# A fused attention, Fourier mix and MLP kernel: the place and time of the mix sums, and the weight steps of one attention turn

## The chip, the cores and the metric

One Trainium2 chip, one core. The metric is device time in microseconds of one launch, lower is better. Of several runs the median is given; one execution is profiled.

## What is computed

Attention with a bias that a small network makes of the distance between positions, then a two-dimensional Fourier transform whose real part is added, a normalisation and an MLP. Batch 4, 8 heads, 576 positions, head size 64, so 512 features; 2048 hidden units.

```
scores = q @ k.T / 8 + bias                     # bias = relu(x @ w1 + b1) @ w2, x from |i - j| and i
x  = softmax(scores) @ v                        # heads side by side: 4 x 576 x 512
u  = x + real(fft(fft(x, axis=1), axis=2))
un = (u - mean(u)) / sqrt(var(u) + 1e-6)        # over the 512 features
out = u + relu(un @ w_ch1) @ w_ch2
```

## The kernel before, in words

Everything is float32; products are made of high and low parts of about 12 bits each (`h` and `l` in tile names), three matmuls for one exact product: hi·hi, hi·lo, lo·hi (`PROD`).

**Attention** (to about 339 us) runs in 16 turns, one for a pair of heads and a batch. Within a turn the order of PE, DVE and ACT is written out by hand in a list of steps, `ORDER`, for all turns but the second (n = 1), which has a list of its own, `SECOND`, and the end, which has `TAIL`. POOL and the DMA queue of SP are ordered by the scheduler that builds the program; a queue runs strictly in order. A step's letter names its work, its digit a block, and a prime each turn that it lags: S scores on PE (`s`), D largest score on DVE (line 290), X exponential on ACT (`p`), T and R transposes on PE into a bank of PSUM (`t`, two banks), VT and VR their evacuation to `pt` (on ACT, or DVE for VR1'), A the products with v on PE (`o`).

W0 to W3 and U0 to U3 turn one 512 KB block of each of the two MLP weight matrices, which arrive as 64-bit floats in `raw`, into float32, one block of each in a turn: W0/U0 on ACT (line 164, `wf`/`uf`), 1 to 3 on DVE (lines 165 to 167), and behind step 3 a store to DRAM (`w_d`, lines 552 and 553). The next turn's `raw` loads are issued on SP when the buffers are free. `load(n)` loads `kT` and `qT` (line 189) when POOL has read the old ones into `kh`, `kl` and `qs` (lines 209, 213).

`keep_bias` (line 326) stores finished bias rows to DRAM (`bias_d`, line 330), six DMAs a call. The last calls, of blocks held back in `later`, stand behind turn n = 0.

**Fourier mix** of a batch b (class `Mix`): sums and differences of rows, `pq` (line 654), and of columns, `ge` (lines 656 and 658), c = 0 for sums and c = 1 for differences; `ge` is split into `gh` and `gl`; PE transforms along the positions (`zp`, line 674, ten matmuls of 320 columns for c and d each, of which part is interleaved) and along the features (`abp`); the result is added to x. For b = 0 all this stands in `TAIL`. For b = 1 to 3 it is part of the stream `pieces`, which is mixed with the dense matmuls of batch b − 1. For b = 1 the sums are made on POOL, otherwise on DVE.

**Dense** (349 to 783 us): `norm` makes the scaled tiles `un`, four of 128x512 (line 773); `flip` transposes them on PE (`ut`, line 787) and splits them into `uh` on ACT (line 789) and `ul` on DVE (line 790). Then for each of 16 blocks f, `up(f)`: splits w1 and w2 into `w1h`, `w1l`, `w2h`, `w2l` (h on ACT, l on POOL), 12 matmuls of 512 columns into `hp` (line 898) and a relu that is split into `hh` and `hl`; `down(f)`: 12 matmuls into the four `acc` (line 912). `end` adds `acc` to x (line 918) and stores. Batch b + 1 is normalised inside batch b; its four transposes stand between the last `down` matmuls of batch b. In the profile batch 0 begins at 349 us, batches 1, 2 and 3 take over near 450, 547 and 645 us, and the matmuls of the two remaining tiles come last, after 722 us. What the scheduler can make early it may put far ahead: before the change the sums of batch 2 were made at 359 to 372 us, inside batch 0.

`un`, `uh` and `ul` live in the pool `unp`, one buffer for each name; `pq` and `ge` of batches 1 to 3 have the pool `fgp`. A tile of the same name waits until the old one is read.

Of the kernel before, what the change touches and what calls it, by code (L numbers as in the profile page):

```python
# [9 lines left out]
F32 = mybir.dt.float32  # L10
# [9 lines left out]
DM, FF, HID = 512, 2048, 32  # L20
P = 128
# [33 lines left out]


SECOND = """
S1 D1 S2 T10' D2 S4 T00' VT10' T01' D4 VT00' VT01' S8' S3 T11' VT11' D8' X8' T02' D3 S6 Q0' VT02' D6 S0 R1'
R0' VR1' X3 VR0' D0 S7 S8 U0 T13' T12' W0 A0' D7 X6 W1 VT13' W2 W3 S5 T04' VT12' T03' D8 U1 Q1' A1' X7 X0
VT03' VT04' X1 D5 U2 U3 X5 A2'  # L60
""".split()


# [69 lines left out]
def body(ctx, tc, a, out):  # L133
    nc = tc.nc
# [270 lines left out]
    with ExitStack() as st:  # L405
# [212 lines left out]
        class Mix:  # L618
# [5 lines left out]
            def buffers(self, c):  # L624
                b = self.b
                if b:
                    pq = fgp.tile([P, 2, DM], F32, tag="pq", name="pq")
                    ge = fgp.tile([P, 3, 256], F32, tag="ge", name="ge")
                    gh = fgp.tile([P, 3, 256], F32R, tag=f"gh{c}", name="gh")
                    gl = fgp.tile([P, 2, 256], F32R, tag=f"gl{c}", name="gl")  # L630
                    self.pq, self.ge[c], self.g[c] = pq, (ge[:, 0:2], ge[:, 2]), (gh, gl)
                    return
# [245 lines left out]
            eng.tensor_tensor(l, src, h.bitcast(F32), ALU.subtract)  # L878
            return h, l

        def dense(ut, tiles, store):
            n = len(tiles)
            N = P * n
            acc = [tps.tile([P, 512], F32, tag="t", name="acc") for t in range(2)]
# [3 lines left out]
            hs, w2s = {}, {}  # L888

            def up(f):  # L890
                wh, wl = split(w1[f // 4][:, f % 4], "w1", nc.gpsimd)
                wf = w2p.tile([P, DM], F32, tag="w2f", name="w2f")
                nc.sync.dma_start(wf, w2_d[f])
                w2s[f] = split(wf, "w2", nc.gpsimd if n == 4 else nc.vector)
                ps = hps.tile([P, 512], F32, tag="h", name="hp")
                mm = [(kb, i, j) for kb in range(4) for i, j in PROD]
                for i, (kb, wi, ui) in enumerate(mm):
                    nc.tensor.matmul(  # L898
                        ps[:, :N], (wh, wl)[wi][:, P * kb:P * kb + P], ut[ui][:, kb, :N],
                        start=i == 0, stop=i == len(mm) - 1)  # L900
# [120 lines left out]
```

## Time and profile before

| | |
|---|---|
| runs | 788.43, 788.58, 784.47 us; median 788.43 |
| profiled execution | 784.86 us, span 783.0 us |
| PE busy | 758.1 us, 97% of the span |
| DVE, ACT, POOL busy | 433.7 (55%), 435.1 (56%), 354.1 us (45%) |
| chain that ended last | PE 88% |
| granted TensorE clock, mean | 0.99 |

The span runs from the first to the last instruction; the execution's time is 1.9 us longer. The chain is followed back from the last instruction to whatever released it, so PE's share of it is the share of time in which nothing but PE set the pace.

### The profile page before, as it was taken

The page shows a single profiled execution, that of the slowest core. Times are in us where ns is not written, and L with a number is a line of the kernel's source. Part 1 is how long each engine was busy: PE and PEld are TensorE (multiplying, and loading weights), DVE is VectorE, ACT ScalarE, POOL GpSimd, SP SyncE. Part 2 cuts the span into 40 slices and gives each one's busy share as a digit, 9 for nine tenths or more (in the row PEclk, how much of TensorE's full clock was granted, in tenths as well). Part 3 has the DMA queues.
Part 4 walks back from the last instruction along what each step waited for, and adds up shares of the span by engine and source line. Part 5 has one row for each costly group of instructions (what it writes and reads, how often), then busy time and mean ns, then how long its engine had stood idle before and what let it go on. Part 6 is the DMA issues. An engine that isn't in the chain of part 4 may idle for free.

```text
span 783.0 us, 13209 instructions
## 1 busy us (share of the span) xinstructions
PE 758.1 (97%) x4786; PEld 617.4 (79%) x4786; DVE 433.7 (55%) x958; ACT 435.1 (56%) x898; POOL 354.1 (45%) x299
## 2 busy tenths in 40 slices
PE   6999899999999999979999999999999999999997
PEld 3567678887788877848888888888888888888896
DVE  7996787987877877587471232713237132111433
ACT  7995888788987888434333333334333342333453
POOL 0003556554663644256554434644355444445442
PEclk9999999999999999979999999999999999999999
DMA  8988989989879743631211121112211112111321
GB/s 220 238 222 228 254 235 297 298 227 283 243 204 284 204 135 92 208 110 28 66 32 50 43 94 54 40 41 64 72 54 41 41 54 95 43 53 54 119 90 61
DMA packets 59488, 103.16 MB, mean 132 GB/s; under 512 B 8768, under 2 KB 28864, under 8 KB 58304
## 3 DMA queue, kind: packets, MB, share of 16 engines
q1 hardware_dynamic: 58672, 98.99, 44.1%
q0 software_dynamic: 288, 3.02, 1.2%
q8 instruction: 37, 0.61, 0.3%
q10 hardware_dynamic: 464, 0.33, 0.1%
q14 instruction: 27, 0.22, 0.1%
HBM read 78.58 MB, written 21.07 MB: 127 GB/s over the span
## 4 chain that ended last, share of the span: by engine, by line
PE 88%; DVE 3%; ACT 3%; DMA 3%; SPq 2%; issue 1%; ACTq 0%; DVEq 0%
PE hp L898 25%; PE acc L912 25%; PE s L272 10%; PE o L462 10%; PE t L441 7%; PE bps L391 4%; PE zp L674 2%; PE abp L693 2%; DMA raw<-m 2%; SPq L330 1%; ACT p L298 1%; PE t L493 1%; DVE un L773 1%; PE ut L787 1%; PE t L431 1%
## 5 line engine op out<-in xcount | busy, mean ns | idle before, releaser
L904 DVE SCALAR_TENSOR_TENSOR hl<-hp,hh 128x512 fp32r<-128x512 f32 (+1 forms) x80 | 50.9, 636 | 229.4 <-ACT hh L903 229.4
L878 POOL TENSOR_TENSOR w1l<-w,w1h 128x512 fp32r<-128x512 f32 x80 | 105.8, 1323 | 106.1 <-ACT w1h L877 104.9
L878 POOL TENSOR_TENSOR w2l<-w2f,w2h 128x512 fp32r<-128x512 f32 x64 | 85.2, 1331 | 102.8 <-ACT w2h L877 102.5
L877 ACT ACTIVATE w1h<-w 128x512 fp32r<-128x512 f32 x80 | 50.4, 632 | 125.6 <-PE hp L898 110.2
L898 PE MATMUL hp<-uh,w1h 128*128 128x512 f32 (+1 forms) x320 | 118.7, 372 | 0.8 <-ACT uh L789 0.8
L898 PE MATMUL hp<-ul,w1h 128*128 128x512 f32 (+1 forms) x320 | 118.7, 371 | 0.7 <-DVE ul L790 0.7
L898 PE MATMUL hp<-uh,w1l 128*128 128x512 f32 (+1 forms) x320 | 118.5, 370 | 0.0
L290 DVE CUSTOM_DVE_ANT_0 p<-s,bias 128x576 f32<-128x576 f32 x128 | 95.1, 754 | 38.8 <-PE s L272 35.3
L877 ACT ACTIVATE w2h<-w2f 128x512 fp32r<-128x512 f32 x80 | 50.6, 632 | 117.8 <-POOL w1l L878 76.3
L912 PE MATMUL acc<-w2l,hh 128*128 128x512 f32 x288 | 112.4, 390 | 0.0
L912 PE MATMUL acc<-w2h,hh 128*128 128x512 f32 x288 | 111.9, 391 | 0.0
L912 PE MATMUL acc<-w2h,hl 128*128 128x512 f32 x288 | 107.4, 391 | 0.0
L272 PE MATMUL s<-kh,qs 128*128 128x288 f32 (+1 forms) x320 | 98.6, 327 | 1.9 <-DVE nm L290 1.8
L298 ACT ACTIVATE p<-p,nm 128x576 f32<-128x576 f32 x128 | 98.0, 772 | 2.8 <-DVE nm L290 1.6
L421 ACT ACTIVATE pt<-t 128x512 f32<-128x512 f32 x141 | 77.9, 594 | 35.9 <-PE t L441 20.0
L272 PE MATMUL s<-kl,qs 128*128 128x288 f32 (+1 forms) x320 | 88.2, 295 | 0.8 <-DVE kl L213 0.8
L462 PE MATMUL o<-pt,v 128*64 128x288 f32 x640 | 85.3, 412 | 0.0
L441 PE MATMUL t<-ident,p 128*128 128x128 f32 x576 | 80.4, 276 | 3.9 <-ACT pt L421 3.7
L209 POOL TENSOR_SCALAR kh<-kT 128x576 fp32r<-128x576 f32 (+1 forms) x28 | 22.8, 831 | 134.6 <-PE s L272 113.5
L272 PEld LDWEIGHTS s<-kh,qs 128*128 128x128 f32 (+1 forms) x320 | 58.4, 183 | 18.7 <-issue 7.0
L441 PEld LDWEIGHTS t<-ident,p 128*128 128x128 f32 x576 | 67.0, 142 | 7.3 <-ACT pt L421 4.8
L898 PEld LDWEIGHTS hp<-ul,w1h 128*128 128x128 f32 x320 | 60.8, 190 | 11.7 <-DVE ul L790 1.5
(136 smaller groups left out, 1387.1 us busy)
## 6 DMA issues: line engine op xcount, KB each, us to landing
w2f<-w_d SPq DMA_DIRECT2D x80, 256.0 KB, 2.6
raw<-m SPq DMA_DIRECT2D x30, 512.0 KB, 5.3
kT<-kT SPq DMA_DIRECT2D x32, 304.0 KB, 4.8
qT<-qT SPq DMA_DIRECT2D x32, 288.0 KB, 4.6
bias_d<-ring SPq DMA_DIRECT2D x54, 144.0 KB, 2.7
bias<-bias_d SPq DMA_DIRECT2D x24, 288.0 KB, 5.4
v<-v SPq DMA_DIRECT2D x16, 320.0 KB, 6.3
out<-x SPq DMA_DIRECT2D x18, 256.0 KB, 2.7
```

The source lines that it names most:

```text
L272: nc.tensor.matmul(ps[:m, c, :CH], qs[:, c0:c0 + m], kk[:, k0 + c * CH:k0 + (c + 1) * CH], start=k == 0, stop=k == 1, skip_group_check=True)
L290: nc.vector.tensor_tensor_reduce(p, bank.pop((n, i))[:, :, :CH], bias, -0.125, 3.0e38, ALU.add, ALU.min, nms[n][:, blk:blk + 1])
L298: nc.scalar.activation(p, p, AF.Exp, bias=nms[n][:, blk:blk + 1], scale=-1.0, accum_out=sums[n][:, blk:blk + 1])
L391: nc.tensor.matmul(ps[32 * t4:32 * t4 + 32, c, :CH], w2[:, int(rev)], h[:, c * CH:(c + 1) * CH], start=True, stop=True, tile_position=(0, ...
L421: nc.scalar.activation(dst, src, AF.Copy)
L441: nc.tensor.transpose(tp[:, 128 * t:128 * t + 128], pb[t].rearrange("p h s -> p (h s)")[:, k0:k0 + 128], ident)
L462: nc.tensor.matmul(os_[u][e, c, :CH], vt[u][:, j, e], pts[u][:, 2 * j + h if j < 4 else 8, c * CH:(c + 1) * CH], start=j == 0, stop=j == 4 ...
L877: nc.scalar.activation(h, src, AF.Copy)
L878: eng.tensor_tensor(l, src, h.bitcast(F32), ALU.subtract)
L898: nc.tensor.matmul(ps[:, :N], (wh, wl)[wi][:, P * kb:P * kb + P], ut[ui][:, kb, :N], start=i == 0, stop=i == len(mm) - 1)
L904: nc.vector.scalar_tensor_tensor(hl[:, :N], ps[:, :N], 0.0, hh[:, :N].bitcast(F32), ALU.max, ALU.subtract)
L912: nc.tensor.matmul(acc[t], h[i][:, P * t:P * t + P], w[j], start=f == 0 and k == 0, stop=f == NF - 1 and k == 2)
```

## The change

Three edits. The sums `pq` and `ge` of batches 1 to 3 are no longer tiles of their own: one tile of the name `un` in `unp` holds them all, for both c. In the first two blocks of batch 0 `w1l` is made on DVE instead of POOL, and the 12 matmuls of the very first block are sorted: four hi·hi, four hi·lo, four lo·hi. In `SECOND` the steps W and U go from the middle to the end, and the held-back `keep_bias` calls from behind turn 0 to behind turn 1.

```
@@ -55,9 +55,9 @@
 
 
 SECOND = """
-S1 D1 S2 T10' D2 S4 T00' VT10' T01' D4 VT00' VT01' S8' S3 T11' VT11' D8' X8' T02' D3 S6 Q0' VT02' D6 S0 R1'
-R0' VR1' X3 VR0' D0 S7 S8 U0 T13' T12' W0 A0' D7 X6 W1 VT13' W2 W3 S5 T04' VT12' T03' D8 U1 Q1' A1' X7 X0
-VT03' VT04' X1 D5 U2 U3 X5 A2'
+S1 D1 S2 T10' D2 S4 T00' VT10' T01' D4 VT00' VT01' S8' S3 T11' VT11' D8' X8' T02' D3 S6 Q0' VT02' D6 S0 R1' R0'
+VR1' X3 VR0' D0 S7 S8 T13' T12' A0' D7 X6 VT13' S5 T04' VT12' T03' D8 Q1' A1' X7 X0 VT03' VT04' X1 D5 X5 A2' W0
+U0 W1 W2 W3 U1 U2 U3
 """.split()
 
 
@@ -587,7 +587,7 @@
             turn_of(n, between)
             if n + 2 < U:
                 load(n + 2)
-            if n == 0:
+            if n == 1:
                 while later:
                     keep_bias()
                 x = xp.tile([P, B, 5, DM], F32, tag="x", name="x")
@@ -624,8 +624,10 @@
             def buffers(self, c):
                 b = self.b
                 if b:
-                    pq = fgp.tile([P, 2, DM], F32, tag="pq", name="pq")
-                    ge = fgp.tile([P, 3, 256], F32, tag="ge", name="ge")
+                    if c == 0:
+                        self.sums = unp.tile([P, 2 * DM + 3 * 256], F32, tag="un", name="pq")
+                    pq = self.sums[:, :2 * DM].rearrange("p (t d) -> p t d", t=2)
+                    ge = self.sums[:, 2 * DM:].rearrange("p (t d) -> p t d", t=3)
                     gh = fgp.tile([P, 3, 256], F32R, tag=f"gh{c}", name="gh")
                     gl = fgp.tile([P, 2, 256], F32R, tag=f"gl{c}", name="gl")
                     self.pq, self.ge[c], self.g[c] = pq, (ge[:, 0:2], ge[:, 2]), (gh, gl)
@@ -878,7 +880,7 @@
             eng.tensor_tensor(l, src, h.bitcast(F32), ALU.subtract)
             return h, l
 
-        def dense(ut, tiles, store):
+        def dense(ut, tiles, store, first=False):
             n = len(tiles)
             N = P * n
             acc = [tps.tile([P, 512], F32, tag="t", name="acc") for t in range(2)]
@@ -888,12 +890,14 @@
             hs, w2s = {}, {}
 
             def up(f):
-                wh, wl = split(w1[f // 4][:, f % 4], "w1", nc.gpsimd)
+                wh, wl = split(w1[f // 4][:, f % 4], "w1", nc.vector if first and f < 2 else nc.gpsimd)
                 wf = w2p.tile([P, DM], F32, tag="w2f", name="w2f")
                 nc.sync.dma_start(wf, w2_d[f])
                 w2s[f] = split(wf, "w2", nc.gpsimd if n == 4 else nc.vector)
                 ps = hps.tile([P, 512], F32, tag="h", name="hp")
                 mm = [(kb, i, j) for kb in range(4) for i, j in PROD]
+                if first and f == 0:
+                    mm.sort(key=lambda m: m[1:])
                 for i, (kb, wi, ui) in enumerate(mm):
                     nc.tensor.matmul(
                         ps[:, :N], (wh, wl)[wi][:, P * kb:P * kb + P], ut[ui][:, kb, :N],
@@ -943,7 +947,7 @@
             def store(t, b=b):
                 nc.sync.dma_start(out[4 * b + t], x[:, b, t])
 
-            main, last_down, end = dense(ut, tl, store)
+            main, last_down, end = dense(ut, tl, store, b == 0)
             if b + 1 < B:
                 tl, un, pcs = prepare(b + 1)
                 n = 4
```

With two lines fewer or more above them, lines shift by 2 to 4: 787 becomes 789, 790 becomes 792, 898 becomes 902, 918 becomes 922, 654 becomes 656.

The queue of SP in the second attention turn, between the load of a first weight piece and the next `rr` stores (the rows with − are the order before, those with + the order now; `raw` of 128x4x128 belongs to W, of 128x512 to U):

```order
-L189 DMA kT<-kT 64x1216 x2
-L189 DMA qT<-qT 64x1152 x2
-L552 DMA w_d<-wf 128x512
-L162 DMA raw<-m 128x4x128
-L487 DMA rr<-rs 64x1 x2
-L553 DMA w_d<-uf 128x512
-L162 DMA raw<-m 128x512
-L196 DMA v<-v 128x5x128
-L189 DMA kT<-kT 64x1216 x2
+L189 DMA kT<-kT 64x1216
+L487 DMA rr<-rs 64x1 x2
+L189 DMA kT<-kT 64x1216
+L189 DMA qT<-qT 64x1152 x2
+L196 DMA v<-v 128x5x128
+L552 DMA w_d<-wf 128x512
+L162 DMA raw<-m 128x4x128
+L189 DMA kT<-kT 64x1216 x2
+L553 DMA w_d<-uf 128x512
+L162 DMA raw<-m 128x512
```

The store of `wf` and the load of the next W block still stand ahead of the last two `kT` loads, but the store of `uf` and the load of the next U block stand behind them now, and the `rr` stores between the two halves of the earlier `kT`.

DVE at the handover from batch 0 to batch 1, before (`hl` belongs to the last blocks of batch 0, `ul` to batch 1, the mix to batch 2):

```order
617 L904 SCALAR_TENSOR_TENSOR hl<-hp,hh 128x512 x8
618 L790 TENSOR_TENSOR ul<-ut,uh 128x4x128 x3
619 L918 TENSOR_TENSOR x<-acc,x 128x512 x2
620 L790 TENSOR_TENSOR ul<-ut,uh 128x4x128
621 L918 TENSOR_TENSOR x<-acc,x 128x512 x2
622 L684 TENSOR_TENSOR z00l<-zp,z00h 128x320
623 L684 TENSOR_TENSOR z01l<-zp,z01h 128x320
624 L666 TENSOR_TENSOR gl<-ge,gh 128x512
```

and now:

```order
602 L908 SCALAR_TENSOR_TENSOR hl<-hp,hh 128x512 x8
603 L792 TENSOR_TENSOR ul<-ut,uh 128x4x128 x3
604 L656 TENSOR_TENSOR pq<-x 128x1024
605 L660 TENSOR_TENSOR pq<-x 128x256
606 L922 TENSOR_TENSOR x<-acc,x 128x512 x2
607 L792 TENSOR_TENSOR ul<-ut,uh 128x4x128
608 L922 TENSOR_TENSOR x<-acc,x 128x512 x2
609 L658 TENSOR_TENSOR pq<-pq 128x512
610 L669 TENSOR_TENSOR gh<-pq,gh 64x256
```

The first sum of batch 2 (`pq` of 128x1024) and the part of `ge` (now named `pq` too) stand ahead of the adds and of the last `ul`. The handover from batch 1 to batch 2 has the same rows, for the sums of batch 3.

PE at the same place, before (the last `acc` of batch 0, then the mix of batch 2, then the first `hp` of batch 1):

```order
1409 L912 MATMUL acc<-w2h,hl 128x512
1410 L674 MATMUL zp<-fs,gh 128x320 x2
1411 L674 MATMUL zp<-fs,gl 128x320
1412 L674 MATMUL zp<-fs,gh 128x320 x2
1413 L674 MATMUL zp<-fs,gl 128x320
1414 L674 MATMUL zp<-fs,gh 128x320 x4
1415 L674 MATMUL zp<-fs,gl 128x320
1416 L674 MATMUL zp<-fs,gh 128x320 x2
1417 L674 MATMUL zp<-fs,gl 128x320
1418 L674 MATMUL zp<-fs,gh 128x320 x2
1419 L898 MATMUL hp<-uh,w1h 128x512
1420 L898 MATMUL hp<-ul,w1h 128x512
```

and now:

```order
1398 L916 MATMUL acc<-w2h,hh 128x512
1399 L916 MATMUL acc<-w2l,hh 128x512
1400 L916 MATMUL acc<-w2h,hl 128x512
1401 L902 MATMUL hp<-uh,w1h 128x512
1402 L902 MATMUL hp<-ul,w1h 128x512
1403 L902 MATMUL hp<-uh,w1l 128x512
```

The `zp` between the last `acc` and the first `hp` are gone from there (they stand later, inside batch 1).

DVE at the start of the dense layers, before:

```order
558 L773 TENSOR_SCALAR un<-x,mv,rs 128x512 x4
559 L790 TENSOR_TENSOR ul<-ut,uh 128x4x128 x3
560 L667 TENSOR_TENSOR gh<-ge,gh 64x256
561 L790 TENSOR_TENSOR ul<-ut,uh 128x4x128
562 L666 TENSOR_TENSOR gl<-ge,gh 128x512
563 L904 SCALAR_TENSOR_TENSOR hl<-hp,hh 128x512
564 L667 TENSOR_TENSOR gh<-ge,gh 64x256
```

and now:

```order
558 L775 TENSOR_SCALAR un<-x,mv,rs 128x512 x4
559 L880 TENSOR_TENSOR w1l<-w_3_4634,w1h 128x512 x2
560 L792 TENSOR_TENSOR ul<-ut,uh 128x4x128 x4
561 L669 TENSOR_TENSOR gh<-pq,gh 64x256
562 L668 TENSOR_TENSOR gl<-pq,gh 128x512
563 L669 TENSOR_TENSOR gh<-pq,gh 64x256
564 L908 SCALAR_TENSOR_TENSOR hl<-hp,hh 128x512 x2
```

Two `w1l` stand between the four `un` and the four `ul`, and no part of the mix stands between the `ul`.

## Rows read from the trace of the kernel before

**Rows 1.** The head of the page: each engine's busy time in us, its share of the span, its instructions.
```profile
PE 758.1 (97%) x4786; PEld 617.4 (79%) x4786; DVE 433.7 (55%) x958; ACT 435.1 (56%) x898; POOL 354.1 (45%) x299
```

**Rows 2.** The list of what PE waited for over the whole execution: engine, line and tile that waited, what it waited for, us in total, times, longest us.
```profile
PE ut L787 <- DVE un L773: 3.8, 4, 1.4
PE t L441 <- ACT pt L421: 3.7, 3, 2.9
```

**Rows 3.** PE in order of time, second and third attention turn: start us, duration us, engine, line, operation, count; in brackets the idle time before it and what ended it.
```profile
82.03 1.14 PE L441 MATMUL t<-ident,p 128*128 128x128 f32 x8 [2.91 <-ACT pt L421]
...
89.49 0.60 PE L441 MATMUL t<-ident,p 128*128 128x128 f32 x4
...
97.79 1.04 PE L441 MATMUL t<-ident,p 128*128 128x128 f32 x8
```

**Rows 4.** PE in order of time, the start of the dense layers (columns as above).
```profile
349.10 0.77 PE L898 MATMUL hp<-uh,w1h 128*128 128x512 f32 x1 [0.77 <-ACT uh L789]
350.19 0.80 PE L898 MATMUL hp<-ul,w1h 128*128 128x512 f32 x1 [0.32 <-DVE ul L790]
350.78 0.63 PE L898 MATMUL hp<-uh,w1l 128*128 128x512 f32 x1
...
353.34 0.63 PE L898 MATMUL hp<-uh,w1l 128*128 128x512 f32 x1
...
357.26 0.74 PE L674 MATMUL zp<-fs,gh 128*128 128x320 f32 x4
```

**Rows 5.** Stretches of the span at the same place: from:to and length, busy us (count) of PE, PEld, DVE, ACT and POOL, granted TensorE clock, DMA share, GB/s.
```profile
343.72:347.13 3.41, 1.49 (x7) 0.72 (x5) 3.41 (x3) 1.50 (x3) 3.08 (x2) 0.50 0.61 230
...
353.96:357.40 3.44, 3.44 (x17) 2.86 (x16) 1.12 (x2) 1.53 (x4) 2.13 (x2) 1.00 0.00 0
```

**Rows 6.** The handover from batch 0 to batch 1 in order of time, PE first, then DVE, then POOL.
```profile
448.14 0.60 PE L787 MATMUL ut<-ident,un 128*128 128x128 f32 x4
...
449.74 0.39 PE L912 MATMUL acc<-w2h,hl 128*128 128x512 f32 x1
449.97 0.45 PE L674 MATMUL zp<-fs,gh 128*128 128x320 f32 x2
...
452.31 0.39 PE L898 MATMUL hp<-uh,w1h 128*128 128x512 f32 x1
...
449.01 1.29 DVE L918 TENSOR_TENSOR x<-acc,x 128x512 f32<-128x512 f32 x2 [2.66 <-PE acc L912]
450.22 0.68 DVE L790 TENSOR_TENSOR ul<-ut,uh 128x512 fp32r<-128x512 f32 x1
...
447.74 1.29 POOL L878 TENSOR_TENSOR w2l<-w2f,w2h 128x512 fp32r<-128x512 f32 x1 [3.01 <-ACT w2h L877]
```

**Rows 7.** ACT in order of time, second and third attention turn.
```profile
79.53 0.66 ACT L164 ACTIVATE uf<-raw 128x512 f32<-128x512 f32 x1 [4.25 <-DMA raw<-m]
...
82.35 0.78 ACT L298 ACTIVATE p<-p,nm 128x576 f32<-128x576 f32 x1
...
85.59 0.78 ACT L298 ACTIVATE p<-p,nm 128x576 f32<-128x576 f32 x1
...
94.27 0.65 ACT L164 ACTIVATE uf<-raw 128x512 f32<-128x512 f32 x1
...
96.16 1.07 ACT L421 ACTIVATE pt<-t 128x512 f32<-128x512 f32 x2
```

**Rows 8.** The DMA queue of SP (SPq: the time is that of issuing) and POOL in the second attention turn, and the row of the DMA list for the transfer issued at 87.05: queue, count, KB each, us from issue to landing.
```profile
68.96 4.38 SPq L330 DMA_DIRECT2D bias_d<-ring  x7
...
87.05 0.43 SPq L162 DMA_DIRECT2D raw<-m  x1
...
90.18 1.14 SPq L189 DMA_DIRECT2D kT<-kT  x2
...
87.21 2.95 POOL L213 TENSOR_TENSOR kl<-kT,kh 128x576 fp32r<-128x576 f32 x2
...
raw<-m SPq DMA_DIRECT2D x1, 512.0 KB, 4.5
```

**Rows 9.** DVE in order of time, second attention turn into the third.
```profile
80.77 0.43 DVE L165 TENSOR_SCALAR raw<-raw 128x512 int32<-128x512 int32 x1 [4.61 <-ACT wf L164]
...
81.96 0.69 DVE L167 SCALAR_TENSOR_TENSOR wf<-wf,raw 128x512 int32<-128x512 int32 x1
...
87.97 0.76 DVE L290 CUSTOM_DVE_ANT_0 p<-s,bias 128x576 f32<-128x576 f32 x1 [1.32 <-PE s L272]
...
88.66 0.45 DVE L423 COPY pt<-t 64x64 f32<-64x64 f32 x2
```

**Rows 10.** The start of the dense layers: DVE in order of time, POOL, and the row on all instructions of line 773 (count, shortest/median/longest ns, first and last start us).
```profile
341.25 5.91 DVE L773 TENSOR_SCALAR un<-x,mv,rs 128x512 f32<-128x512 f32 x4
347.08 1.87 DVE L790 TENSOR_TENSOR ul<-ut,uh 128x512 fp32r<-128x512 f32 x3
...
344.47 2.41 POOL L654 TENSOR_TENSOR pq<-x 128x1024 f32<-128x1024 f32 x1
...
L773 DVE TENSOR_SCALAR un<-x,mv,rs x18: 533/883/2566, 341.3 to 644.0; 128x512 f32<-128x512 f32 x18
```

**Rows 11.** DVE, one of the sums made ahead inside batch 0.
```profile
365.15 1.21 DVE L654 TENSOR_TENSOR pq<-x 128x1024 f32<-128x1024 f32 x1
```

**Rows 12.** DVE at the handover from batch 1 to batch 2.
```profile
546.86 0.68 DVE L790 TENSOR_TENSOR ul<-ut,uh 128x512 fp32r<-128x512 f32 x1
```

More of the change, by code (lines that the diff above doesn't have):

```diff
@@ L57 @@
 SECOND = """
-S1 D1 S2 T10' D2 S4 T00' VT10' T01' D4 VT00' VT01' S8' S3 T11' VT11' D8' X8' T02' D3 S6 Q0' VT02' D6 S0 R1'
-R0' VR1' X3 VR0' D0 S7 S8 U0 T13' T12' W0 A0' D7 X6 W1 VT13' W2 W3 S5 T04' VT12' T03' D8 U1 Q1' A1' X7 X0
-VT03' VT04' X1 D5 U2 U3 X5 A2'
+S1 D1 S2 T10' D2 S4 T00' VT10' T01' D4 VT00' VT01' S8' S3 T11' VT11' D8' X8' T02' D3 S6 Q0' VT02' D6 S0 R1' R0'
+VR1' X3 VR0' D0 S7 S8 T13' T12' A0' D7 X6 VT13' S5 T04' VT12' T03' D8 Q1' A1' X7 X0 VT03' VT04' X1 D5 X5 A2' W0
+U0 W1 W2 W3 U1 U2 U3
 """.split()
@@ L589, in body @@
                 load(n + 2)
-            if n == 0:
+            if n == 1:
                 while later:
@@ L626, in buffers @@
                 if b:
-                    pq = fgp.tile([P, 2, DM], F32, tag="pq", name="pq")
-                    ge = fgp.tile([P, 3, 256], F32, tag="ge", name="ge")
+                    if c == 0:
+                        self.sums = unp.tile([P, 2 * DM + 3 * 256], F32, tag="un", name="pq")
+                    pq = self.sums[:, :2 * DM].rearrange("p (t d) -> p t d", t=2)
+                    ge = self.sums[:, 2 * DM:].rearrange("p (t d) -> p t d", t=3)
                     gh = fgp.tile([P, 3, 256], F32R, tag=f"gh{c}", name="gh")
@@ L879, in split, with dense @@
             return h, l
-        def dense(ut, tiles, store):
+        def dense(ut, tiles, store, first=False):
             n = len(tiles)
@@ L890, in up @@
             def up(f):
-                wh, wl = split(w1[f // 4][:, f % 4], "w1", nc.gpsimd)
+                wh, wl = split(w1[f // 4][:, f % 4], "w1", nc.vector if first and f < 2 else nc.gpsimd)
                 wf = w2p.tile([P, DM], F32, tag="w2f", name="w2f")
@@ L896, in up @@
                 mm = [(kb, i, j) for kb in range(4) for i, j in PROD]
+                if first and f == 0:
+                    mm.sort(key=lambda m: m[1:])
                 for i, (kb, wi, ui) in enumerate(mm):
@@ L944, in store @@
                 nc.sync.dma_start(out[4 * b + t], x[:, b, t])
-            main, last_down, end = dense(ut, tl, store)
+            main, last_down, end = dense(ut, tl, store, b == 0)
             if b + 1 < B:
```

## The prediction, made before the changed kernel was timed

> **What bounds the kernel now.** I read the page first: PE is busy 758.1 us, 97% of the span [rows 1]. So the end moves only by what PE gains or loses as idle time or as slower matmuls, about 25 us in all. Next I read PE's list of waits: the two entries that this change reaches are `ut` for DVE's `un` (3.8 us in four waits, at the start of the dense layers) and `t` for ACT's `pt` (3.7 us, the longest of them 2.9 us) [rows 2]. Then PE's rows around each edit. In the second attention turn (n = 1) one stall of 2.91 us stands at 82.03 [rows 3]. At the dense start there are gaps ahead of the `ut` transposes, and behind them PE ran at a granted clock of 0.50, that is 1.2 GHz, with 0.43 us from one `hp` matmul to the next (350.78 to 353.34, six steps) [rows 4, 5] instead of the 0.23 between two matmuls of that size at full clock [rows 6]. Third, a place that has no wait today: where batch 0 is handed over to batch 1, PE's rows follow each other without an idle time in brackets [rows 6]. What is full can only lose.
>
> **The baseline.** The sum is made against the profiled execution, 784.86 us (span 783.0 plus 1.9 around it). The runs beside it took 788.43, 788.58 and 784.47 us, so the profile lies at their low end, 3.6 below the median. I put the sum on the mean of the four, 786.6. A change under 0.5% (3.9 us) can't be told from none here, as these four spread that far by themselves.
>
> **Part 1, the second turn.** Removed: ACT's `uf`/`wf` steps from the middle of its queue. Before, `uf` held ACT for 4.25 us until its `raw` landed, behind it stood the exponentials and the evacuations `pt` that free PE's transposes, and PE lost 2.91 us [rows 3, 7]. With W0 and U0 behind X5, ACT runs on and that stall goes: −2.9. The raw transfers also pass six of the seven `bias_d` stores of 4.38 us, 3.8 us earlier [rows 8], and nothing in this turn wants them that early any more; this costs and gives nothing.
>
> Added: the six VectorE steps W1 to U3 now stand in one piece ahead of D1 of the next turn. ACT needs 4.0 us from X7 to the end of X5 (82.35 to 86.4) [rows 7]; unblocked it starts X6 as soon as D7 allows, near 76.2, X7 4.25 less 0.2 ahead of before, near 78.3, X5 ends near 82.4 and `wf` near 83.0. W1 to W3 took 1.9 us (80.77 to 82.65) [rows 9], and I give U1 to U3 the same: U3 ends near 86.8. Then come D1 and the small `pt` copies (88.66 plus 0.45, ending 1.14 behind the start of D1) [rows 9], so that the transpose bank of R1' is free near 88.0 to 88.3. PE, now 2.9 us ahead, reaches the first `t` of the turn, which wants that bank, near 86.6 (before: 89.49) [rows 3]. It waits 1.3 to 2.0; I take 1.6.
>
> Moved on SP: the store of `uf` and the `raw` load of the next weights stood at 87.05, ahead of the two `kT` loads at 90.18. Now they stand behind them, and these wait until POOL has read the old `kT`, at 90.16 (87.21 plus 2.95), and take 1.14 to issue [rows 8]. One half of the earlier `kT` also goes behind the two `rr` stores, so POOL comes 0 to 1.2 later. Thus `kT` goes out at 90.2 to 91.3, `raw` 1.5 later at 91.7 to 92.8, and with the landing of 4.5 us of that same load [rows 8] it is there at 96.2 to 97.3, later if the burst is contended. In the third turn the order is the old one: ACT's `uf` stands in the middle and before started at 94.27 without a wait [rows 7]; with PE 1.3 ahead ACT reaches it near 93.0. From `uf` to the first of the two `pt` took 2.45 us (94.27 to 96.7, the first half of the pair at 96.16) and PE's next `t` came at 97.79 [rows 3, 7], now 96.5: PE stays unhurt only if raw lands by 94.1. Landed at 97, it loses 2.9. So the stall comes back one turn later with about its old size, as ACT waits about 4 us again: I take +3.0, bounds 0 (transfer in time) and 4.5. Part 1 together: −2.9 + 1.6 + 3.0 = **+1.7**, between −1.6 and +3.6.
>
> **Part 2, the dense start.** Removed from POOL: the sum `pq` that ran beside VectorE's last mix steps, and the sums and `w1l` parts that ran beside the four `un`. Those took 5.91 us, while the shortest `un` took 533 ns [rows 10]; without POOL beside them 2.0, so `un` ends near 343.25 instead of 347.16. Added on VectorE: two `w1l`, 0.65 each by the pitch of `ul` (three in 1.87) [rows 10], to 344.55. Three `ul` follow, to 346.4, and the first `hp`, which wants the bank of the third `ut`, starts near 346.45 instead of 349.10. It is sorted to take four hi·hi products first, which covers the last `ul`; the second `hp`, which waited 0.32 for `ul` [rows 4], then has no wait. The added `w2l` go to POOL's idle time before `un`, and the sums of batch 1 behind the last transposes. POOL's two `pq` of 2.41 [rows 10] and the small sums end near 352; the 24 `hp` matmuls cover that, and only if they ended at 351.9 would the `zp` behind them wait, for a `gl` that comes near 352.8: 0.9.
>
> The clock decides the rest. It returned to 1.00 at 353.96, 4.9 us after the first `hp` [rows 4, 5]. If the return keeps its distance from the first `hp`, about 11 of the 24 matmuls run at 0.43 and 13 at 0.23: they end at 354.2 instead of 357.26, a gain of 3.1. If the clock never falls they end at 351.9 (gain 5.4); if it returns at 353.96 all the same, near 355.4 (gain 1.8). I take **−3.2**, nearest the row. The Trainium skill (TensorE: Matmul & The Clock Gate, What's actually happening) says that the throttled clock is the default state which activity releases, and that the number of slow matmuls differs from run to run; by it any of my three ends may come, which no run here shows yet.
>
> **Part 3, the two full handovers.** The sums of batches 2 and 3 share the memory of `un`, so they can't start before the last `ut` transpose has read it. Before, they had been made long ahead, and 16 `zp` matmuls stood behind the last `acc`, 449.97 to 452.31; under them VectorE did two adds (1.29 from 449.01) and the last `ul` (450.22 to 450.90) [rows 6]. Now those `zp` are gone from there, the first `hp` follows the last `acc` at 449.97, and on VectorE `pq` and a third of `ge` stand ahead of the adds and of `ul`. The transposes end at 448.74 (448.14 plus 0.60), so `pq` can start at 448.8; POOL's `w2l` (447.74 plus 1.29) holds it until 449.03 [rows 6]; it takes 1.21 [rows 11] to 450.24; the part of `ge`, a quarter of its size, 0.3 to 0.5; two adds 1.2; `ul` 0.68: 452.4 to 452.7. PE's second `hp` wants that `ul`, and would have started at 450.2. A stall of 2.2 to 2.5, and the zp come later at their full price. The handover from batch 1 to batch 2 has the same order and distances (its `ul` at 546.86) [rows 12]. Twice 2.25: **+4.5**; bounds 3 (`pq` at half its price) and 5.5. A stall of 2.9 at 82 did not lower the clock in the profile, so I add nothing for that. By the Trainium skill (SBUF — State Buffer, Who interferes with whom) whichever of a GpSimd operation and a VectorE one with two SBUF inputs starts first holds the shared ports and the other waits; without that hold `pq` would end 0.2 sooner and the sum be 4.1. The `un` agree with it: beside POOL they took three times their time [rows 10].
>
> **The sum.** +1.7 − 3.2 + 4.5 = **+3.0**: 787.9 for the profiled execution, 789.6 on the mean of the four. That is within 0.5%, on the slow side.
>
> **Rivals.**
> 1. *Slower: POOL wins the race at the dense start.* `pq` of batch 1 may start when the last `ut` is done, near 343.9; VectorE's second `w1l` wants to start near 343.9 as well. If POOL is first, `w1l` and the four `ul` behind it wait out its 2.41 us [rows 10]. For it: both are within 0.2 us. Against it: PE's transpose waits for the last `un`, which frees VectorE 0.6 earlier. Price +2.4: 792.0, slower. It decides once `un` ends over 0.3 us behind my time. Chance 0.15.
> 2. *The stall isn't carried on.* If the raw load of the third turn lands by 94, part 1 is −1.3 and the time 786.6, the same as before. For it: `kT` may land sooner with the raw loads out of the way. Against it: the queue is in order, and 1.5 us of issue and 4.5 of landing stand behind POOL's 90.16. Chance 0.15.
> 3. *The clock stays up at the dense start.* 2.2 better, 787.4. For it: three fewer gaps between the `ut`. Against it: PE still has some 2.5 us without work ahead of the first `hp`. Chance 0.12.
> 4. *Faster: the handovers hold, as the last `ul` needn't wait.* If POOL and the earlier `ul` leave `pq` under the last `acc`, with each stall under 0.5, part 3 is +1 and with rival 3 or 2 the time falls to 783 to 784, with both to 781. Against it: the transpose that frees the memory ends 1.2 before the last `acc`, and 2.5 us of VectorE work stand in between. Chance 0.08.
>
> The forecast itself keeps 0.50, with its own range 787 to 792; its upper quarter lies beyond 0.5%. Slower by over 0.5%: 0.15 for rival 1, 0.14 for the upper part of the forecast, 0.02 for several bounds at once, 0.31; faster 0.12, rival 4 and half of what no case covers; the same 0.57. Range: from rival 4's upper end and rival 2's lower bound to rival 1 with a late raw: 784.5 to 793.5.
>
> **What will show it.** Right: no `pt` wait of 2.9 near 79, but a wait of 1 to 2 for DVE's `pt` near 85 to 88 and a `raw` wait of ACT near 93 with 2 to 4 us of PE behind it; four `un` in about 2 us and the first `hp` some 2.6 earlier; two new waits of `hp` for `ul` of about 2.25 at the handovers to batches 1 and 2 and none of that size at the one to batch 3. Wrong if those two waits are missing, if `raw` lands before ACT asks, or if a `w1l` on VectorE takes over 2 us.

## The result and the profile after

The changed kernel took 793.06 us in the median of 6 runs (792.07 to 794.65), the kernel before beside it 788.31 us (784.47 to 788.95): a ratio of 1.0077, with a 95% interval of 1.0057 to 1.0097. It is slower by more than the 0.5% that can be told from no change.

PE's busy time rose by 0.7 us [rows 1], its wait for `un` fell from 3.8 to 1.0 us, and two other waits grew: `t` for `pt` from 3.7 to 6.8 [rows 2], and `hp` for `ul` from 0.7 to 6.7. The head of the page and PE's list of waits, after:

```profile
PE 758.8 (96%) x4786; PEld 617.2 (78%) x4786; DVE 430.6 (54%) x960; ACT 435.0 (55%) x898; POOL 349.3 (44%) x297
```
```profile
PE t L441 <- ACT pt L421: 6.8, 4, 4.3
PE hp L902 <- DVE ul L792: 6.7, 4, 2.4
...
PE ut L789 <- DVE un L775: 1.0, 1, 1.0
```

**The third attention turn**, in order of time: SP's queue, then ACT, then PE, after; in the second fence PE at the same place before.

```profile
91.06 1.11 SPq L189 DMA_DIRECT2D kT<-kT  x2
92.84 0.43 SPq L162 DMA_DIRECT2D raw<-m  x1
...
98.22 0.66 ACT L164 ACTIVATE uf<-raw 128x512 f32<-128x512 f32 x1 [5.40 <-DMA raw<-m]
...
87.36 0.66 PE L441 MATMUL t<-ident,p 128*128 128x128 f32 x4 [0.92 <-ACT pt L421]
...
89.43 1.03 PE L441 MATMUL t<-ident,p 128*128 128x128 f32 x8
...
100.72 1.97 PE L441 MATMUL t<-ident,p 128*128 128x128 f32 x8 [4.33 <-ACT pt L421]
...
102.61 5.44 PE L462 MATMUL o<-pt,v 128*64 128x288 f32 x32
```
```profile
90.98 1.04 PE L441 MATMUL t<-ident,p 128*128 128x128 f32 x8
...
98.75 4.10 PE L462 MATMUL o<-pt,v 128*64 128x288 f32 x32
```

The stall of 2.91 at 82 [rows 3] is gone, but `raw` is issued at 92.84 instead of 87.05 [rows 8], behind `kT`; ACT waits 5.40 us for it, and PE 4.33 for the `pt` behind. The `t` that came at 97.79 [rows 3] comes at 100.72, and 32 `o` matmuls take 5.44 us instead of 4.10.

Stretches of the span after (columns as in [rows 5]; the granted clock follows POOL's busy time): the third turn, and the handovers to batch 1 and batch 2.

```profile
98.50:102.00 3.50, 1.28 (x6) 1.29 (x7) 2.47 (x6) 3.50 (x9) 1.16 (x2) 0.50 0.27 62
102.00:105.50 3.50, 3.50 (x18) 1.80 (x18) 3.47 (x7) 3.44 (x9) 3.50 (x3) 0.52 0.71 227
...
453.50:457.00 3.50, 3.50 (x9) 2.76 (x10) 3.44 (x6) 0.63 (x1) 0.00 (x0) 0.51 0.91 294
553.50:557.00 3.50, 3.06 (x13) 2.53 (x14) 3.44 (x6) 0.63 (x1) 0.35 (x1) 1.00 0.95 330
```

The clock stood at its lower level, 1.2 GHz, from 98.5 to 105.5 (from 105.5 to 109.0 the view has 1.00), and behind the first handover, but not behind the second.

**The start of the dense layers** after, DVE, then POOL, then PE:

```profile
346.42 1.91 DVE L775 TENSOR_SCALAR un<-x,mv,rs 128x512 f32<-128x512 f32 x4
348.24 1.29 DVE L880 TENSOR_TENSOR w1l<-w,w1h 128x512 fp32r<-128x512 f32 x2
349.44 2.48 DVE L792 TENSOR_TENSOR ul<-ut,uh 128x512 fp32r<-128x512 f32 x4
...
349.17 2.57 POOL L656 TENSOR_TENSOR pq<-x 128x1024 f32<-128x1024 f32 x1 [3.79 <-PE ut L789]
...
351.47 2.04 PE L902 MATMUL hp<-uh,w1h 128*128 128x512 f32 x4 [2.44 <-DVE ul L792]
...
358.47 0.74 PE L676 MATMUL zp<-fs,gh 128*128 128x320 f32 x4
```

The four `un` take 1.91 us instead of 5.91 [rows 10] and the two `w1l` 0.65 each. The second `w1l` starts at 348.84 and POOL's `pq` at 349.17, 0.33 behind it. From the first `un` to the first `zp` it is 12.05 us; before it was 16.01 (341.25 to 357.26) [rows 4, 10].

**The handovers** to batch 1 (DVE, then PE) and to batch 2 (PE), after:

```profile
449.95 1.33 DVE L656 TENSOR_TENSOR pq<-x 128x1024 f32<-128x1024 f32 x1 [2.42 <-PE ut L789]
451.20 0.41 DVE L660 TENSOR_TENSOR pq<-x 128x256 f32<-128x256 f32 x1
451.54 1.28 DVE L922 TENSOR_TENSOR x<-acc,x 128x512 f32<-128x512 f32 x2
452.73 0.68 DVE L792 TENSOR_TENSOR ul<-ut,uh 128x512 fp32r<-128x512 f32 x1
...
451.14 0.39 PE L902 MATMUL hp<-uh,w1h 128*128 128x512 f32 x1
453.46 0.77 PE L902 MATMUL hp<-ul,w1h 128*128 128x512 f32 x1 [1.93 <-DVE ul L792]
...
551.62 0.39 PE L902 MATMUL hp<-uh,w1h 128*128 128x512 f32 x1
553.94 0.51 PE L902 MATMUL hp<-ul,w1h 128*128 128x512 f32 x1 [1.93 <-DVE ul L792]
```

`pq` and a third of `ge` (the row of 128x256) stand ahead of the adds and of `ul`, and each second `hp` comes 2.32 us behind the first, 2.09 more than a pitch of 0.23. [Rows 6] had no wait there.

**Where the time went**, by marks in the two traces. The end of the third turn comes 5.2 us later; the dense start gives back 3.95 (16.01 less 12.05); the handovers cost 5.8 (twice 2.09, and 1.6 for eight matmuls at a pitch of 0.43). That is +7.0; the spans differ by 7.3 (790.3 and 783.0). The medians differ by less, 4.75, as the profile before lay 3.5 below the median of its runs and the one after 1.0.

### The profile page after: what moved, and what is told of

It reads as the page before. It is cut to its first block, busy times and chain, and to the rows that moved or that the text cites. A ratio compares the mean times of both kernels' runs of the same rounds, so it can differ in the third digit from the quotient of the medians.

```text
span 790.3 us, 13197 instructions
## 1 busy us (share of the span) xinstructions
PE 758.8 (96%) x4786; PEld 617.2 (78%) x4786; DVE 430.6 (54%) x960; ACT 435.0 (55%) x898; POOL 349.3 (44%) x297
## 4 chain that ended last, share of the span: by engine, by line
PE 87%; DVE 5%; ACT 4%; DMA 3%; issue 1%; ACTq 0%; DVEq 0%; SPq 0%
PE hp L902 25%; PE acc L916 24%; PE s L272 10%; PE o L462 9%; PE t L441 7%; PE bps L391 3%; PE zp L676 2%; PE abp L695 2%; ACT p L298 1%; DMA bias<-ring 1%; PE t L493 1%; DMA v<-v 1%; PE t L431 1%; DVE hd L371 1%; DMA raw<-m 1%
## 5 line engine op out<-in xcount | busy, mean ns | idle before, releaser
L880 POOL TENSOR_TENSOR w1l<-w,w1h 128x512 fp32r<-128x512 f32 x78 | 101.6, 1303 | 105.2 <-ACT w1h L879 105.2
L880 POOL TENSOR_TENSOR w2l<-w2f,w2h 128x512 fp32r<-128x512 f32 x64 | 82.9, 1295 | 113.7 <-ACT w2h L879 113.5
```

## The experiments

**before_again and after_again: the two kernels, unchanged, profiled a second time.**

> The kernel before once more, unchanged, for a second profile of it. If the spread of its runs (785 to 792 us) comes from stretches in which the granted clock is 0.50, the stretches stand at other places or number one or two more or fewer than in the first profile, with 1.7 us for each of 3.4 us; if it comes from the DMAs, the waits for raw and kT differ by as much.

> The changed kernel once more, unchanged. The wait of PE for pt in the third turn (4.3 us) and the two waits of hp for ul (1.9 us) come again within 0.5 us, since the program's order makes them; the stretches at half the clock behind them (6.8 us behind the first, 3.4 behind the second, none behind the third) need not come at the same places.

Measured: 786.2 and 790.8 us. In before_again PE's stall at the same place was only 1.72, but the clock fell behind it (PE, then the stretch); in the profile of before, with a stall of 2.91, the same stretch ran at 1.00 (second fence). Six profiles here have the second turn as it was, with the bias stores behind turn 0. In them this stall was 1.72 to 2.91 us, and the clock fell behind it at 1.72, 1.99 and 2.32 (before_again, hold_hand, dense_part) but not at 2.09, 2.34 and 2.91 (own_sums, sums_hold, before). As both the stall and the stretch differ between the two profiles of before, the two cases of the expectation are not told apart; the spans are 784.3 and 783.0 us.

```profile
80.78 1.14 PE L441 MATMUL t<-ident,p 128*128 128x128 f32 x8 [1.72 <-ACT pt L421]
...
82.00:86.00 4.00, 4.00 (x20) 2.06 (x20) 3.75 (x10) 4.00 (x11) 2.46 (x3) 0.57 1.01 262
```
```profile
82.00:86.00 4.00, 3.97 (x32) 2.62 (x34) 3.89 (x11) 4.00 (x10) 1.11 (x1) 1.00 1.03 245
```

In after_again both handover waits of 1.93 came again, with the lower clock behind the first only (453.0 to 456.5). The wait of 4.3 in the third turn did not: `raw` landed no sooner (98.91), but PE had by then lost 1.55 at 90.8 and a stretch at 1.2 GHz (91.0 to 94.5), so that it was less early for it. ACT and PE of after_again:

```profile
98.91 0.68 ACT L164 ACTIVATE uf<-raw 128x512 f32<-128x512 f32 x1 [1.74 <-DMA raw<-m]
...
90.80 0.40 PE L272 MATMUL s<-kh,qs 128*128 128x288 f32 x1 [1.55 <-DVE nm L290]
...
101.44 1.14 PE L441 MATMUL t<-ident,p 128*128 128x128 f32 x8 [0.67 <-ACT pt L421]
```

The expectation missed this: the loss by the end of that turn, 3.8 us against the profile of before, was made of other waits than in the first profile.

**turn_part: the second turn's new list and the later `keep_bias()`, without the dense edits.** (Against before: the SECOND list of the change, and `if n == 1`.)

> Only the edits of the attention turns: the second turn's steps W and U at its end, and the held-back bias stores behind turn 1. Theory (the stall is carried on): the 2.9 us wait of PE for pt near 79 is gone, but the U load stands behind the kT loads, so ACT waits over 5 us for raw near 93 and PE about 4.3 us for pt near 96; behind that wait the granted clock falls to 0.50 and the next 36 to 40 matmuls take about 2.3 us longer. Together 4 to 5.5 us slower than before, ratio 1.005 to 1.007. Rival (the loss in the third turn belongs to the whole change, through other places in memory or another phase): no raw wait over 1 us in the third turn, time as before or up to 3 us faster, ratio 0.996 to 1.001.

Measured: 793.37 us, ratio 1.0055 (1.0035 to 1.0075): the theory's time, with smaller waits than it named. PE waited 1.56 for `nm` at 90.27 and ran at 1.2 GHz from 90.5 to 94.0, as in after_again; then `uf` started at 99.42 after a wait of 2.79, and the `t` behind it at 101.93 after one of 1.73. In three profiles with these edits that `t` follows the landing of `raw` by 2.5 us: 98.22 and 100.72, 98.91 and 101.44, 99.42 and 101.93, whatever PE lost ahead of it.

**dense_part: the dense edits alone.** (Against before: the edits from line 624 on.)

> Only the edits of the dense layers: sums in the place of the scaled tiles, two low weight parts on VectorE, the first twelve matmuls sorted. Theory: the dense start is 3 to 4 us shorter, each of the two handovers has a wait of hp for ul of 1.9 us where two matmuls are 2.1 apart beyond their pitch, and a handover behind which the clock falls to 0.50 costs 1.6 more. Together between 0 and 3.5 us slower than before, ratio 1.000 to 1.0045. Rival (the start gains nothing that lasts, the handovers cost more than their waits): 4 us or more slower, ratio above 1.005.

Measured: 788.1 us, 1.0009 (0.9987 to 1.0032), in the theory's range. The clock did not fall at the dense start, which was worth 5.4 there, and both handover waits came, with the lower clock behind the first (450.0 to 454.0). The two parts add up within their intervals (0.55% and 0.09%, against 0.77%): the second turn makes the loss.

**steps_late and bias_late: the turn's two edits apart.**

steps_late has the change's SECOND list alone, bias_late this alone:

```diff
-            if n == 0:
+            if n == 1:
                 while later:
                     keep_bias()
```

> Only the step list of the second turn; the held-back bias stores stay behind turn 0. Theory (the place of the U steps at the end puts its load behind kT): the same wait of ACT for raw in the third turn and the same loss as with both edits, 4 to 5.5 us, ratio 1.005 to 1.007. Rival (the later bias stores hold up the queue and the kT half, and these make the load late): the raw wait is under 3 us and PE's stall under 2, time within 2 us of before, ratio 0.998 to 1.003.

> Only the held-back bias stores behind turn 1; the steps stay in the middle of the second turn. Theory (the raw loads of the second turn are late because six bias stores stand ahead of them): both loads are issued 3.8 us earlier, raw lands near 75.7, ACT waits under 1 us for it and PE's 2.9 us wait for pt near 79 is gone, with no wait put in its place: 2.5 to 3 us faster, ratio 0.996 to 0.997. Rival (the landing is set by the load on the DMA queues, not by the issue): raw lands 1 us earlier at most, PE still waits 2 us or more, ratio 0.998 to 1.001.

steps_late: 792.34 us, 1.0054 (1.0034 to 1.0074). The time was the theory's, but without its wait: `raw` was there when ACT asked (98.18), and the loss stood ahead of it. So the list of steps makes the loss without the later bias stores. DVE's last steps, POOL and PE:

```profile
86.02 0.96 DVE L165 TENSOR_SCALAR raw<-raw 128x512 int32<-128x512 int32 x1
87.02 1.77 DVE L166 SCALAR_TENSOR_TENSOR raw<-raw 128x512 int32<-128x512 int32 x1
88.82 1.91 DVE L167 SCALAR_TENSOR_TENSOR uf<-uf,raw 128x512 int32<-128x512 int32 x1
...
86.67 3.51 POOL L213 TENSOR_TENSOR kl<-kT,kh 128x576 fp32r<-128x576 f32 x2
...
91.46 0.40 PE L272 MATMUL s<-kh,qs 128*128 128x288 f32 x1 [2.78 <-DVE nm L290]
```

The same three operations take 0.43, 0.69 and 0.69 us undisturbed (the first and the third, on the other block, in [rows 9]). U1 to U3 took 0.96, 1.77 and 1.91 beside POOL's split of the next `kT`, whose first part ran from 84.86 and whose second part is shown; D1 waited behind them, PE 2.78 for its `nm`, and the clock fell behind that wait (93.0 to 96.5). In the profile of after POOL began at 86.61 instead, 1.6 behind U1, and the three took 0.43, 0.69 and 0.69: the same program has the collision in after_again and not there.

bias_late: 788.04 us, 1.0000 (0.9977 to 1.0024). By itself the later `keep_bias()` removes the stall, as the theory had it (`uf` starts at 74.89 without a wait), and PE is 2.2 us ahead by the end of the third and fourth turns. It loses 1.6 of that in the fifth, where `raw` stands behind the saved biases' loads and PE waits 1.32 for `pt`; at the first `un` nothing is left (341.30, before 341.25). So the time is the rival's.

**third_late and asks_later: the third turn's steps moved too.** Both add a list for n = 2 to turn_part. The diff is that of third_late, and its last two lines are the list's end in asks_later against it.

```diff
+THIRD = """
...
+S5 T04' VT12' T03' D8 A1' X7 X0 VT03' VT04' X1 D5 X5 A2' W0 U0 W1 W2 W3 U1 U2 U3
+""".split()
...
-            for i, w in enumerate(SECOND if n == 1 else ORDER):
+            for i, w in enumerate(SECOND if n == 1 else THIRD if n == 2 else ORDER):
...
-S5 T04' VT12' T03' D8 A1' X7 X0 VT03' VT04' X1 D5 X5 A2' W0 U0 W1 W2 W3 U1 U2 U3
+S5 T04' VT12' T03' D8 A1' X7 X0 VT03' VT04' U0 W0 W1 W2 W3 X1 D5 U1 U2 U3 X5 A2'
```

> The edits of the attention turns alone, and the third turn too has its steps W and U at its end. Theory (late steps hand their loads and their VectorE work on to the next turn): the wait of PE for pt in the third turn is under 0.5 us, but ahead of D1 of the fourth turn the six VectorE steps stand in one piece beside POOL and PE waits 2 us or more there; the time is within 2 us of that with the second turn alone late, so 2.5 to 6 us slower than before, ratio 1.003 to 1.0075. Rival (the loss is made once, by the third turn's list that asks for raw in its middle): no such wait in the fourth turn, 0 to 2 us slower than before, ratio 1.000 to 1.0025.

> This is turn_part with one edit more: in the third turn alone the steps U0, W0 and W1 to W3, which use the raw weights, stand behind VT04' instead of ahead of T13', so that ACT asks for raw some 4 us later than in turn_part; U1 to U3 stand ahead of X5. The second turn's late block (W1 to U3 on VectorE ahead of the third turn's D1) is left as in turn_part. Theory (the load that stands late in its queue costs the larger part: ACT waits for it with the evacuations behind it): no wait of uf over 1 us in the third turn and no wait of PE for pt behind it (turn_part 2.79 and 1.73), the end of the third turn 2 to 4 us earlier than in turn_part, unless the fourth turn's load is now asked for too late in its turn, which would show as a wait of uf there; ratio to before 1.000 to 1.003. Rival (the late VectorE block alone costs it: PE waits for nm and pt at 88 to 91 and the clock falls behind that): the waits at 88 to 92 stay, the half-clock stretch behind them too, the end of the third turn stays 3 to 5 us behind before, ratio 1.004 to 1.007.

third_late: 795.51 us, 1.0114 (1.0085 to 1.0143), beyond the theory's bound. asks_later: 794.26 us, 1.0087 (1.0060 to 1.0113), which neither side expected. Its rows (PE, DVE, POOL, PE again, third turn into the fourth) tell the two causes apart all the same:

```profile
98.14 1.03 PE L448 MATMUL t<-ident,p 128*128 128x128 f32 x8
...
104.62 0.96 DVE L172 TENSOR_SCALAR raw<-raw 128x512 int32<-128x512 int32 x1
105.61 1.92 DVE L173 SCALAR_TENSOR_TENSOR raw<-raw 128x512 int32<-128x512 int32 x1
107.57 1.77 DVE L174 SCALAR_TENSOR_TENSOR uf<-uf,raw 128x512 int32<-128x512 int32 x1
...
103.46 3.53 POOL L220 TENSOR_TENSOR kl<-kT,kh 128x576 fp32r<-128x576 f32 x2
...
110.68 1.12 PE L438 MATMUL t<-ident,pr 128*128 128x128 f32 x4 [4.54 <-DVE x L514]
```

ACT found `raw` landed, and the `t` came at 98.14, 3.8 us earlier than in turn_part. Half of that, 1.9, is the wait for the late load that is gone; the other half had been gained ahead of it, as U1 to U3 of the second turn met POOL for less time here (0.42, 1.08 and 1.09) and the clock stayed up. An estimate of what the late load would have cost this profile: `raw` landed at 99.0 (issued at 93.40, 5.6 on the way), so with the old place of the steps the `t` would have come near 101.5, 3.4 later. Up to there the theory holds. But then U1 to U3 ran beside POOL's split for the fourth turn, D1 came late, PE waited 4.54 and the clock fell (110.5 to 114.0). In third_late the same wait was 5.93. So steps at a turn's end cost by themselves, and here more than in the second turn (waits of 4.54 and 5.93 against 2.78 in steps_late).

**own_sums: the two moved parts without the moved sums.** Against before, with the sums left in tiles of their own:

```diff
-                wh, wl = split(w1[f // 4][:, f % 4], "w1", nc.gpsimd)
+                wh, wl = split(w1[f // 4][:, f % 4], "w1", nc.vector if first and f < 2 else nc.gpsimd)
...
+                if first and f == 0:
+                    mm.sort(key=lambda m: m[1:])
```

> The two low weight parts on VectorE and the sorted first matmuls alone; the sums keep tiles of their own. Theory (what made the scaled tiles slow were the sums and low parts that POOL made beside them): POOL still makes the sums of batch 1 beside the scaled tiles, so these take 3.5 us or more instead of 1.9, the dense start gains 1 to 2.5 us, no wait at the handovers: ratio 0.997 to 0.999. Rival (the low parts alone did it): the scaled tiles take 2 us and the start gains 4 us, ratio 0.994 to 0.996.

Measured: 785.0 us, 0.9985 (0.9965 to 1.0005). The four `un` took 1.91, as the rival had it; but POOL's sum now ran beside the last norm, where a step on four columns took 1.95 us instead of 0.17, PE waited 1.99 and the clock was low from 340 to 350.5. The time was the theory's, the mark the rival's. DVE, then POOL, then PE:

```profile
337.82 1.95 DVE L766 SCALAR_TENSOR_TENSOR rs<-rs 128x4 f32<-128x4 f32 x1
339.80 0.17 DVE L767 SCALAR_TENSOR_TENSOR rs<-rs 128x4 f32<-128x4 f32 x1
...
337.39 2.35 POOL L654 TENSOR_TENSOR pq<-x 128x1024 f32<-128x1024 f32 x1
...
340.81 0.47 PE L497 MATMUL t<-ident,ot 128*128 128x128 f32 x1 [1.99 <-DVE x L507]
```

**hold_hand: the dense edits, with the handover's order mended.** A one-column operation reads `un` and the last `ul`: the sums, in the memory of `un`, must wait for this reader, and it waits for `ul`. DVE's order at the handovers is the one written in the code.

```diff
+                if n == 4 and t == 3:
+                    nc.vector.tensor_tensor(
+                        fw2.tile([P, 1], F32, tag="hold", name="hold"), un[0][:, 3, 0:1],
+                        ul[:, 0, 384:385].bitcast(F32), ALU.add)
...
+            with tc.manual_schedule(engines={DVE_}):
+                run(fl + last_down)
+                end()
```

> The edits of the dense layers alone, and besides: at each handover the four low parts ul come first on VectorE, then a one-column operation that reads the scaled tile and ul, then the adds; so the sums can't start ahead of the last ul. Theory (the handovers lose because the sums stand ahead of the last ul): both waits of hp for ul, 1.9 us each, shrink to under 0.3, the clock stays up there, the gain of the dense start (4 to 5.4 us) remains: 3 to 5 us faster than before, ratio 0.9935 to 0.9965. Rival (the handovers are slower because the zp matmuls no longer cover them, whatever VectorE does first): waits of 1 us or more remain for another producer, ratio 0.998 to 1.001.

Measured: 782.1 us beside 786.77, 0.9949 (0.9927 to 0.9971). DVE, then PE, at the handover to batch 1:

```profile
449.08 0.69 DVE L792 TENSOR_TENSOR ul<-ut,uh 128x512 fp32r<-128x512 f32 x1 [3.04 <-ACT uh L791]
449.80 0.16 DVE L794 TENSOR_TENSOR hold<-un,ul 128x1 f32<-128x1 f32 x1
449.88 2.48 DVE L926 TENSOR_TENSOR x<-acc,x 128x512 f32<-128x512 f32 x4
452.27 1.22 DVE L656 TENSOR_TENSOR pq<-x 128x1024 f32<-128x1024 f32 x1
...
449.87 0.45 PE L906 MATMUL hp<-ul,w1h 128*128 128x512 f32 x1
```

The last `ul` is ahead of the adds and of the sums, and no `hp` waits at a handover, for `ul` or anything else, though the `zp` stand inside batch 1 here too: the theory holds, and the kernel is 4.7 us faster than before.

**hold_hand_bias: the same with the edit of bias_late.**

> The dense layers as in the version that holds the sums behind the last ul, and the held-back bias stores behind turn 1, the second turn's list as before the change. Theory (what the second turn gains with earlier raw loads is given back by the fifth turn, whose raw load stands behind bias loads): 4 to 5 us faster than before as without the later bias stores, ratio 0.993 to 0.9965. Rival (the gain of 2 us lasts where the dense layers are in order): ratio under 0.993.

Measured: 783.93 us, 0.9958 (0.9942 to 0.9974). PE was 2.1 us ahead of the profile of before until the fourth turn; in the fifth ACT waited 3.67 for `raw`, PE 2.61 for `pt`, and a stretch at 1.2 GHz followed (131.5 to 135.5). At the end of the sixth it was 2.4 behind: given back, as expected, and no gain over hold_hand.

**sums_hold: hold_hand without `w1l` on VectorE and without the sort.**

```diff
-                wh, wl = split(w1[f // 4][:, f % 4], "w1", nc.vector if first and f < 2 else nc.gpsimd)
+                wh, wl = split(w1[f // 4][:, f % 4], "w1", nc.gpsimd)
...
-                if first and f == 0:
-                    mm.sort(key=lambda m: m[1:])
```

> As the version that holds the sums behind the last ul, but the first two w1l stay on POOL and the first matmuls unsorted. Theory (the dense start gains mainly because POOL no longer makes sums beside the scaled tiles): the four scaled tiles run beside the two w1l of POOL and take 3 to 4.5 us, the first hp 1.5 to 2.5 us earlier than before; 2 to 4 us faster than before, ratio 0.995 to 0.9975. Rival (the low parts on VectorE are what gains): within 1 us of before, ratio 0.9985 to 1.001.

Measured: 781.38 us, 0.9935 (0.9913 to 0.9956), better than the theory's bound; the interval overlaps that of hold_hand, so the two are not told apart. POOL's `w1l` slow the `un` a little (2.92 instead of 1.91) but end at 344.08, 3.6 us ahead of the end of the last `ul`, which PE waits for anyway:

```profile
342.36 2.92 DVE L775 TENSOR_SCALAR un<-x,mv,rs 128x512 f32<-128x512 f32 x4
345.19 2.47 DVE L792 TENSOR_TENSOR ul<-ut,uh 128x512 fp32r<-128x512 f32 x4
...
341.40 2.68 POOL L884 TENSOR_TENSOR w1l<-w,w1h 128x512 fp32r<-128x512 f32 x2 [0.38 <-ACT w1h L883]
```

The clock stayed up at the dense start in this profile, while it fell in that of hold_hand (350.0 to 353.5). So the gain needs only that POOL does not make the sums there; the two moved parts add none that can be told.

## Why the prediction was wrong

It said 789.6, a loss within 0.5%; measured were 793.06, a loss of 0.77%, inside the range. The stall carried into the third turn, the shorter dense start and the two handover waits came at the places named. Two steps failed: the carried stall was sized too small, and the clock behind a stall was put at nothing. The baseline adds 1.7 (786.6 taken, 788.3 measured).

- **The second turn, −2.9 + 1.6: right in this profile, in part by luck.** PE reached its second `t` of the third turn 1.55 us ahead (89.43 against 90.98 before); the sum had 1.3. But it waited 0.92 for ACT's `pt` (87.36) and 0.25 for `nm`, not for DVE's `pt`. In turn_part and after_again it was 1.6 and 2.1 behind, as U1 to U3 met POOL's split. The prediction gave them their undisturbed 1.9 us and did not look at POOL, though it read POOL's work beside the `un` in [rows 10]. The −2.9 is also the largest of the six stalls seen at that place.
- **The carried stall, +3.0: the step that failed.** `kT` at 91.06 and `raw` at 92.84 lie at the late end of the times given. The landing was taken as 4.5 us from the one transfer of [rows 8]; the page's median over the 30 loads is 5.3, before and after, and here it was 5.4 (92.84 to 98.22). PE's wait became 4.33, near the upper bound of 4.5.
- **"A stall of 2.9 at 82 did not lower the clock in the profile, so I add nothing": the other step that failed.** This was said of the handovers; for the carried stall the sum had nothing for the clock either. The third turn lost 2.3 us to it: from the start of the `t` to that of the `o` it was 1.89 us (0.96 before), and the 32 `o` took 5.44 (4.10 before). The first handover lost 1.6. One profile with no fall had been taken for the rule: the clock fell behind that very stall in three of six profiles.
- **The dense start, −3.2: right in mechanism and side, small in size.** 3.95 in the profile, where the clock was back some 3 us behind the first `hp` instead of the 4.9 that the sum kept (which gives 3.1 by its own working). It was 5.4, the upper end, in dense_part and after_again, where the clock stayed up. This is rival 3, in two of the five profiles with these edits: in hold_hand and hold_hand_bias it fell too. Rival 1 did not come, by 0.33 us; and the four `ul` beside POOL's `pq` took 2.48, 0.62 each as in [rows 10], so they would not have waited it out. The Trainium skill (TensorE: Matmul & The Clock Gate, What's actually happening) says that the number of slow matmuls differs from run to run, and these profiles agree.
- **The handovers, +4.5: right.** 2.09 each where 2.25 were taken, and besides the clock's 1.6 at one. hold_hand shows the cause: with `ul` ahead of the sums the wait is gone and the kernel faster than before.

The `un`, which the prediction put to the rule on VectorE operations with two SBUF inputs, have one tensor input; that POOL slows them is shown by the rows alone (5.91 beside it, 1.91 without). The chances of its five cases add up to 1.00, which leaves nothing for "what no case covers".

How a load 6 us later in its queue, U1 to U3 beside POOL, and the clock share the second turn's 0.55% (turn_part) can't be fixed to a number: the shares change from profile to profile, while the sum stays at 3.8 to 5.2 us by the end of the third turn (after, after_again, turn_part, steps_late, against the profile of before).

## What to carry to other kernels

Work moved to a turn's end meets what the next turn starts with: look there for the other engine on the same memory, and for every load that goes behind a waiting one in the same queue. Take a transfer's time as the median of its group, and take a stall under load as possibly followed by a stretch at 1.2 GHz, about 1.7 us here (32 `o` in 5.79 instead of 4.10 in before_again), whichever way one profile went. When tiles share memory, the last reader's place sets the order behind it; a one-column operation that ties the new tile to the later reader cost 0.16 us and turned a loss at the handovers into none.

## What the runs showed of the hardware

- The same wait of 1.93 us stands at two handovers of after, after_again and dense_part. The clock fell behind the first in all three and behind the second in none; what differs between the places is not settled. A wait of 1.55 to 1.56 for `nm` near 90 was followed by a fall in after_again and turn_part and by none in third_late.
- int32 steps with all operands in SBUF slow beside POOL's split of `kT`: 0.43 us became 0.91 to 0.96 for the step with one input, and 0.69 up to 1.92 for those with two (turn_part, steps_late, asks_later). `ul`, with one of its inputs in PSUM, kept its 0.62 beside POOL's `pq` (after).
- The Trainium skill (SBUF — State Buffer, Who interferes with whom) says that of a VectorE operation with two SBUF inputs and a GpSimd one that reads SBUF, the one that starts first holds the shared ports and the other waits. own_sums agrees: the four-column step of 1.95 us, which has two inputs, ended at 339.77, and POOL's `pq`, begun 0.43 ahead of it, at 339.74.
- A gain in an early turn was given back at a later load of the same queue: 1.6 of 2.2 us at 127 in bias_late, and all of 2.1 at 128 in hold_hand_bias.
